# Inverse norms on VectorE by Newton steps instead of logarithms and exponentials on ScalarE, in a fused attention and feed-forward kernel

## The chip, the cores and the metric

The kernel runs on one core of a Trainium2 chip. The metric is the device time of one execution in microseconds (us). A core has five engines that run side by side and meet at semaphores: PE (TensorE, matrix products), DVE (VectorE), ACT (ScalarE, with activation tables that must be loaded), POOL (GpSimd) and SP (SyncE, which here only issues DMAs). Each engine works through its own list in order; an instruction that waits holds up all that stand behind it on its engine.

## The reference

The program is cosine attention followed by a feed-forward block with the gate h·cos(h):

```python
def _attn_ref(q, k, v, tau):                      # (8, 12, 448, 64) each
    q_n = q / (np.linalg.norm(q, axis=-1, keepdims=True) + 1e-06)
    k_n = k / (np.linalg.norm(k, axis=-1, keepdims=True) + 1e-06)
    scores = np.matmul(q_n, k_n.transpose(0, 1, 3, 2)) / tau
    scores = scores - np.max(scores, axis=-1, keepdims=True)
    attn = np.exp(scores)
    attn = attn / (np.sum(attn, axis=-1, keepdims=True) + 1e-09)
    return np.matmul(attn, v).astype(np.float32)

x = attn_out.transpose(0, 2, 1, 3).reshape(8 * 448, 768)
h = x @ w_in                                      # 768 x 2048
out = (h * np.cos(h)) @ w_out                     # 2048 x 768
```

The part of interest is the first two lines: each row of 64 numbers of q and k is divided by its norm plus 1e-6.

## The kernel before

**Quads.** The 96 heads are worked off as 24 quads of four heads (three quads make one of the eight batches). A quad holds 28 row norms per partition for q and k together: 14 for each, in the tile `n2` (sums of squares) and `rr` (inverse norms). Both tiles, and the scratch tile `nrm`, have two buffers, used by even and odd quads.

**Way of a quad through the engines.** SP loads `Qf` and `Kf` (L398). POOL squares them (`square`, L450), DVE sums the squares over 64 (L454, into `n2`). `inverse` (L461) makes `rr` from `n2`. POOL multiplies (`scale`, L501, into `Qn` and `Kn`), SP transposes both by DMA (`turn`, L544), and PE can then run the seven groups of scores of this quad (L560). ACT takes the exponential of each group into `E` (L567), PE multiplies `E` with V (L577), and DVE empties the one pair of PSUM banks used for that into `AVs` (L586) before the next quad may use it. Every second quad `sums` (L630) adds up the rows of `E` on PE, ACT inverts them by a logarithm and an exponential (L649, L651) and issues their store (L652), SP reads them back spread over the partitions (`R`, L658), and POOL (one quad: DVE) forms the normalised `xT` (L662).

**Inverse norm before the change.** All quads begin with ln and exp(0.5·) on ACT (L480, L483): that is the norm. Quads 1 to 7 (`FAST = 7`) then add 1e-6 by a reduction over pairs on DVE (L486) and take the reciprocal there (L489). Quad 0 and quads 8 to 23 stay on ACT: ln(norm + 1e-6) and exp(-·) (L491, L493). So ACT runs two instructions for each of quads 1 to 7 and four for each of quads 8 to 23.

**Stages.** The first three quads form a prologue whose order is written out by hand. From then on the program alternates, for each batch of 448 tokens, between a stage of the first product (`m1_part` and `m1`: PE L676, then per pair of 128 rows of h: ACT L689, DVE L691, ACT L693, DVE L695, which together compute h·cos(h) into `gT`), and a stage in which the second product (`m2`, L704, with its result copied out by DVE at L722) is mixed with the attention of the next quads: 5, 4, 3, 3, 3 and 3 of them, and none in the last two. PE pairs of L676 use four double PSUM banks in turn, so PE writes pair 4 only when DVE has finished L695 of pair 0; which pair frees which bank is given by `at_bank` (L921): for the first batch pairs 0, 2, 1 and 3 free the banks of pairs 4, 5, 6 and 7.

**Order of work.** PE's order is the order of the program text. The order on ACT, DVE, POOL and SP comes from a planner (class `Planner`) that goes through the operations with an assumed duration for each (the second argument of `op`), a latency after it (DVE 0.085) and a hop to the waiting engine (DVE 0.035), and at each point takes the operation that can start first; among those that can start together the one that is needed earliest goes first, and one needed over 1 us (`WORTH`) earlier is preferred. `lead` makes an operation count as needed so much earlier: 5 us for norms of quads 5 and on. An operation waits for an earlier one of its own engine by semaphore too, PE excepted.

**Where norms are asked for.** Quads 3 and 4 at L910 and L912, behind the last ACT instruction of the prologue (L609); that is at the start of the first m1 stage. Quad 5 at L981, in the first attention stage. Quads 6 to 23 by `begin` (L750), called at the first group of the quad two before, behind the exponential of the last group ahead of it.

Of the kernel before, what the change touches and what calls it, by code (L numbers as in the profile page):

```python
# [9 lines left out]
ALU = mybir.AluOpType  # L10
# [3 lines left out]
I32 = mybir.dt.int32  # L14
# [7 lines left out]
class Planner:  # L22
# [10 lines left out]
    FIRST, LAST = 1.2, 0.8  # L33
# [9 lines left out]
    def op(self, eng, dur, fn, r=(), w=(), after=(), dma=None, moves=0, mode="f", chain=None, keep=False, lead=0.0):  # L43
        o = Op()
        o.i, o.eng, o.dur, o.fn, o.dma, o.moves, o.mode, o.chain = (
            len(self.ops), eng, dur, fn, dma, moves, mode, chain)
        o.lat = self.FIRST + moves + self.LAST if dma else self.LAT[eng]
        o.behind, o.lead = None, lead
        if keep or self.strict and eng in ("act", "dve", "pool"):
            o.behind, self.tail[eng] = self.tail.get(eng), o  # L50
        o.reads, o.writes = tuple(r), tuple(w)
        deps = {a.i for a in after if a is not None}
        for x in o.reads:
            if x in self.last_write:
                deps.add(self.last_write[x].i)
        for x in o.writes:
            if x in self.last_write:
                deps.add(self.last_write[x].i)
            deps.update(p.i for p in self.readers.get(x, ()))
        deps.discard(o.i)  # L60
        o.deps = sorted(deps)
        for x in o.reads:
            self.readers.setdefault(x, []).append(o)
        for x in o.writes:
            self.last_write[x] = o
            self.readers[x] = []
        self.ops.append(o)
        return o
# [203 lines left out]
def bass_cosine_attention__then__act_gcu_kernel(  # L272
# [12 lines left out]
    NJ = S // D  # L285
# [6 lines left out]
    FIRST = 3  # L292
# [8 lines left out]
    def ring(name, n, shape, dt):  # L301
        return [sb("%s%d" % (name, i), shape, dt) for i in range(n)]
# [10 lines left out]
    n2 = ring("n2", 2, [128, 4 * NJ], F32)  # L313
    nrm = ring("nrm", 2, [128, 4 * NJ, 2], F32)
    rr = ring("rr", 2, [128, 4 * NJ], F32)
# [26 lines left out]
    op = P.op  # L342
# [24 lines left out]
    def table(m):  # L367
        if mode[0] == m:
            return
        mode[0] = m  # L370
        op("act", 1.3, lambda e: e.add_instruction(mybir.InstLoadActFuncSet(
            name=nc.get_next_instruction_name(), act_func_set_id={"exp": 6, "sin": 9}[m], engine=e.engine)),
           w=["table"])

    def act(m, dur, fn, r=(), w=(), **kw):
        table(m)
        return op("act", dur, fn, r=[*r, "table"], w=w, **kw)

    ALL = ((0, NJ),)
# [3 lines left out]
    def cut(kind, u, part):  # L383

        return [(kind, u, i) for i, (j0, j1) in enumerate(CELLS) if part[0] < j1 and j0 < part[1]]
# [39 lines left out]
        return pool_dma(0.79, lambda e: e.dma_start(W2.ap()[:, 8 * i:8 * i + 8, HW * hf:HW * hf + HW], src),  # L425
                 w=[("W2", i, hf)], dma=("W2", i, hf), moves=5.18)

    H, NLEAD, FAST = 2 * NJ, 5.0, 7
    SPARE = FIRST + 3

    def jr(t, w, part, off=0):
# [2 lines left out]
    def square(qd, w, eng, part=ALL[0], after=()):  # L434
# [23 lines left out]

        return add

    def inverse(qd, w0, w1, part=ALL[0], after=()):  # L461

        u = qd % 2
        ws = range(w0, w1)

        def cells(name):
            return [c for w in ws for c in cut("%s%d" % (name, w), u, part)]

        j0, j1 = part
        rows = [NJ, 2 * (w1 - w0)], [1, j1 - j0]
        if part == ALL[0]:
            rows = [[1, H * (w1 - w0)]]
        t, o = (bass.AP(x[u], w0 * H + j0, [[2 * H, 128], *rows]) for x in (n2, rr))
        wide = [[2 * a, b] for a, b in rows]
        z = bass.AP(nrm[u], 2 * (w0 * H + j0), [[4 * H, 128], *wide])
        both = bass.AP(nrm[u], 2 * (w0 * H + j0), [[4 * H, 128], *wide, [1, 2]])
        lead = NLEAD * (qd > FIRST + 1)
        act("exp", 0.12, lambda e: e.activation(z, t, ACT.Ln, bias=1e-30, scale=1.0), r=cells("n2"), w=cells("nrm"),  # L480
            after=after, lead=lead)
        yield
        act("exp", 0.12, lambda e: e.activation(z, z, ACT.Exp, bias=0.0, scale=0.5), r=cells("nrm"), w=cells("nrm"), lead=lead)  # L483
        yield
        if 0 < qd <= FAST:
            op("dve", 0.13, lambda e: e.tensor_reduce(out=o, in_=both, axis=AX.X, op=ALU.add), r=cells("nrm") + ["eps"],  # L486
               w=cells("rr"), lead=lead)
            yield
            op("dve", 0.27, lambda e: e.reciprocal(o, o), r=cells("rr"), w=cells("rr"), lead=lead)  # L489
            return  # L490
        act("exp", 0.12, lambda e: e.activation(z, z, ACT.Ln, bias=1e-6, scale=1.0), r=cells("nrm"), w=cells("nrm"), lead=lead)  # L491
        yield
        act("exp", 0.12, lambda e: e.activation(o, z, ACT.Exp, bias=0.0, scale=-1.0), r=cells("nrm"), w=cells("rr"), lead=lead)  # L493
# [15 lines left out]
    def norm_b(qd, eng="pool", after=()):  # L509
        for _ in inverse(qd, 0, 2, after=after):  # L510
            pass
        for w in range(2):
            last = scale(qd, w, eng)
        return last
# [278 lines left out]

    square(0, 1, "dve", KP[0])()
    key = inverse(0, 1, 2, KP[0])
    adds = []
    for part in QP:
# [10 lines left out]
    scale(0, 1, "dve", KP[0])  # L808
    adds[2]()
    query, key = inverse(0, 0, 1), inverse(0, 1, 2, KP[1])  # L810
    for x in (query, query, query, query, key, key, key, key):
        next(x, None)
# [213 lines left out]
```

## Time and profile before

| | |
|---|---|
| median of 3 runs | 441.71 us (440.83 to 442.9) |
| the profiled execution | 441.8 us, span 439.6 us, mean granted TensorE clock 0.992 |
| PE busy | 420.1 us (96%) |
| ACT busy | 315.3 us (72%), 434 instructions |
| DVE busy | 254.7 us (58%), 300 instructions |
| POOL busy | 211.2 us (48%), 145 instructions |
| ln and exp of the norms on 28 columns (L480, L483, L491, L493) | 23 + 23 + 16 + 16 instructions, 229, 228, 228 and 226 ns each |
| reduction and reciprocal on DVE (L486, L489) | 7 + 7 instructions, 200 and 326 ns each |
| exponentials of the scores (L567) | 168 instructions, 144.8 us in all |
| loads of activation tables (L371) | 16, 1283 ns each |

"Busy" counts the union of an engine's instructions; overlapping neighbours on DVE and ACT start about 0.1 us before the one ahead has ended. The time outside the span (2.2 us in the profiled execution) is start and end of the program. A line such as "PE PS L577 <- ACT E L567: 1.8, 7, 0.4" says that PE stood idle before L577 for 1.8 us in 7 places, the longest 0.4 us, and that ACT's L567 ended each of these waits.

### The profile page before, as it was taken

The page shows a single profiled execution, that of the slowest core. Times are in us where ns is not written, and L with a number is a line of the kernel's source. Part 1 is how long each engine was busy: PE and PEld are TensorE (multiplying, and loading weights), DVE is VectorE, ACT ScalarE, POOL GpSimd, SP SyncE. Part 2 cuts the span into 40 slices and gives each one's busy share as a digit, 9 for nine tenths or more (in the row PEclk, how much of TensorE's full clock was granted, in tenths as well). Part 3 has the DMA queues.
Part 4 walks back from the last instruction along what each step waited for, and adds up shares of the span by engine and source line. Part 5 has one row for each costly group of instructions (what it writes and reads, how often), then busy time and mean ns, then how long its engine had stood idle before and what let it go on. Part 6 is the DMA issues. An engine that isn't in the chain of part 4 may idle for free.

```text
span 439.6 us, 8369 instructions
## 1 busy us (share of the span) xinstructions
PE 420.1 (96%) x3544; PEld 204.6 (47%) x3544; DVE 254.7 (58%) x300; ACT 315.3 (72%) x434; POOL 211.2 (48%) x145
## 2 busy tenths in 40 slices
PE   5989999988999999999999999999999999999996
PEld 5444543324544345434554444434454445555553
DVE  4674995347863449823696419923585237825931
ACT  4798789896788877788688667888678666815700
POOL 3878727869167694376637682148633120030000
PEclk9699999999999999999999999999999999999999
DMA  7999996999919969188933994075912611051022
GB/s 253 233 251 227 261 196 92 233 223 208 146 41 240 240 172 213 37 206 123 265 89 80 241 210 141 1 171 150 259 35 48 154 43 30 0 159 36 1 71 73
DMA packets 70941, 64.34 MB, mean 146 GB/s; under 512 B 40100, under 2 KB 63224, under 8 KB 70904
## 3 DMA queue, kind: packets, MB, share of 16 engines
q1 hardware_dynamic: 57824, 51.30, 46.6%
q0 software_dynamic: 12288, 11.80, 18.2%
q10 hardware_dynamic: 792, 0.71, 0.5%
q8 instruction: 28, 0.46, 0.4%
q14 instruction: 9, 0.07, 0.1%
HBM read 55.25 MB, written 11.16 MB: 151 GB/s over the span
## 4 chain that ended last, share of the span: by engine, by line
PE 83%; ACT 9%; DVE 3%; issue 2%; POOL 2%; ACTq 1%; POOLq 0%
PE PS L676 33%; PE PS L704 31%; PE PS L560 7%; PE PS L577 6%; ACT E L567 6%; PE PS L642 4%; DVE n L454 1%; ACT Zs L651 1%; ACT Zs L649 1%; ACTq L652 1%; PE PS L599 1%; PE PS L623 1%; POOL xT L662 0%; DVE gT L695 0%; ACT ar L609 0%
## 5 line engine op out<-in xcount | busy, mean ns | idle before, releaser
L704 PE MATMUL PS<-W,gT 128*128 128x384 bf16 x896 | 163.4, 327 | 1.1 <-DVE osb L722 1.0
L567 ACT ACTIVATE E<-PS 128x896 bf16<-128x896 f32 x168 | 144.8, 916 | 27.0 <-PE PS L560 23.8
L676 PE MATMUL PS<-xT,W 128*128 128x448 bf16 x768 | 147.7, 353 | 1.2 <-POOL xT L662 1.2
L704 PEld LDWEIGHTS PS<-W,gT 128*128 128x128 bf16 x896 | 80.1, 98 | 80.7 <-issue 29.0
L676 PEld LDWEIGHTS PS<-xT,W 128*128 128x128 bf16 x768 | 74.3, 98 | 72.0 <-POOL xT L662 1.6
L689 ACT ACTIVATE ar<-PS 128x896 int32<-128x896 f32 x64 | 58.2, 910 | 45.1 <-PE PS L676 45.1
L691 DVE SCALAR_TENSOR_TENSOR ar<-ar,PS 128x896 f32<-128x896 int32 x64 | 69.2, 1083 | 29.0 <-ACT ar L689 29.0
L722 DVE COPY osb<-PS 128x384 f32<-128x384 f32 x54 | 29.2, 554 | 86.6 <-PE PS L704 86.5
L662 POOL TENSOR_TENSOR xT<-AVs,R 128x896 bf16<-128x896 f32 x20 | 41.4, 2088 | 67.5 <-DMA R<-rscr 67.4
L695 DVE TENSOR_TENSOR gT<-PS,ar 128x896 bf16<-128x896 f32 x64 | 69.6, 1088 | 1.5 <-ACT ar L693 1.0
L693 ACT ACTIVATE ar<-ar 128x896 f32<-128x896 f32 x64 | 60.6, 946 | 13.1 <-DVE ar L691 13.1
L560 PE MATMUL PS<-qT,kT 64*64 64x448 bf16 x672 | 62.1, 368 | 4.9 <-ACT E L567 4.0
L450 POOL TENSOR_TENSOR sqq<-Qf 128x896 bf16<-128x896 f32 x21 | 35.3, 1679 | 49.3 <-DVE n L454 40.9
L577 PE MATMUL PS<-E,Vb 64*64 64x448 bf16 x672 | 50.4, 353 | 2.1 <-ACT E L567 1.8
L501 POOL TENSOR_TENSOR Qn<-Qf,rr 128x896 bf16<-128x896 f32 x21 | 35.4, 1687 | 29.6 <-ACT rr L493 25.1
L450 POOL TENSOR_TENSOR sqk<-Kf 128x896 bf16<-128x896 f32 (+1 forms) x22 | 36.5, 1659 | 25.9 <-DVE n L454 17.9
L586 DVE COPY AVs<-PS 128x896 f32<-128x896 f32 x21 | 22.8, 1087 | 29.6 <-PE PS L577 29.6
L501 POOL TENSOR_TENSOR Kn<-Kf,rr 128x896 bf16<-128x896 f32 (+1 forms) x22 | 37.5, 1705 | 0.5 <-DVE Qn L501 0.5
L560 PEld LDWEIGHTS PS<-qT,kT 64*64 64x64 bf16 x672 | 18.6, 105 | 38.4 <-issue 15.6
L454 DVE TENSOR_REDUCE n<-sqq 128x14 f32<-128x896 bf16 (+2 forms) x24 | 24.9, 1037 | 5.8 <-POOL sqq L450 5.7
L454 DVE TENSOR_REDUCE n<-sqk 128x14 f32<-128x896 bf16 (+2 forms) x24 | 25.0, 1040 | 5.4 <-POOL sqk L450 5.4
L577 PEld LDWEIGHTS PS<-E,Vb 64*64 64x64 bf16 x672 | 19.3, 106 | 17.5 <-ACT E L567 10.6
(53 smaller groups left out, 175.9 us busy)
## 6 DMA issues: line engine op xcount, KB each, us to landing
Qf<-in_q_dram SPq DMA_DIRECT2D x24, 448.0 KB, 6.0
out_dram<-osb SPq DMA_DIRECT2D x54, 192.0 KB, 3.6
Kf<-in_k_dram SPq DMA_DIRECT2D x23, 448.0 KB, 7.2
R<-rscr SPq DMA_DIRECT2D x42, 224.0 KB, 4.2
Vb<-in_v_dram POOLq DMA_DIRECT2D x24, 224.0 KB, 6.7
W<-in_moe_w_in_dram POOLq DMA_DIRECT2D x4, 768.0 KB, 18.3
W<-in_moe_w_out_dram POOLq DMA_DIRECT2D x4, 768.0 KB, 31.9
Kf<-in_k_dram ACTq DMA_DIRECT2D x1, 320.0 KB, 6.2
```

Source lines behind the costliest of these rows:

```text
L450: op(eng, (1.68 if eng == "pool" else 1.05) * n, lambda e: e.tensor_tensor(dst, src, src, ALU.mult), r=cut(nm + "f", s, part), w=at, after ...
L454: return op("dve", 0.07 + 0.95 * n, lambda e: e.tensor_reduce(out=n2[u].ap()[:, H * w:H * w + H] if part == ALL[0] else jr(n2[u], w, part) ...
L501: lambda e: e.tensor_tensor(n[u].ap()[:, j0:j1].rearrange("p j r d -> p r j d"), f[s].ap()[:, :, j0:j1], rb, ALU.mult),
L560: ins = e.matmul(bank(bs + r, S, 64 * a, 64 * a + 64), kT[u].ap()[64 * r:64 * r + 64, j, a, :], qT[u].ap()[64 * r:64 * r + 64, :, a, :], s ...
L567: act("exp", 0.875, lambda e: e.activation(E[es].ap(), two(bs), ACT.Exp, bias=0.0, scale=INV_TAU), r=pair(bs), w=[("E", es)], chain="E")
L577: ins = e.matmul(bank((X, Y)[a], S, 64 * r, 64 * r + 64), Vb[vs].ap()[64 * a:64 * a + 64, r, j, :], E[es].ap()[64 * a:64 * a + 64, r, :], ...
L676: ins = e.matmul(bank(bk + i2), W1.ap()[:, i, 128 * nb:128 * nb + 128], xT[c % 2].ap()[:, i, :], start=(i == 0), stop=(i == NKC - 1))
L689: op("act", 0.815, lambda e: e.activation(ar[s].ap().bitcast(I32), two(bk), ACT.Identity, bias=0.25, scale=INV2PI), r=bs, w=[("ar", s)])
L691: op("dve", 1.005, lambda e: e.scalar_tensor_tensor(ar[s].ap(), ar[s].ap().bitcast(I32), -2.0 * math.pi, two(bk), ALU.mult, ALU.add), r=bs ...
L693: act("sin", 0.86, lambda e: e.activation(ar[s].ap(), ar[s].ap(), ACT.Sin, bias=GUARD * math.pi / 2.0, scale=GUARD), r=[("ar", s)], w=[("a ...
L695: op("dve", 1.01, lambda e: e.tensor_tensor(gT.ap()[:, 2 * pr:2 * pr + 2, col:col + S], two(bk), ar[s].ap(), ALU.mult), r=bs + [("ar", s)] ...
L704: ins = e.matmul(bank(bk, HW), gT.ap()[:, f, col:col + 128], W2.ap()[:, f, HW * h:HW * h + HW], start=(f == 0), stop=(f == NNB - 1))
```

## The change

Quads 3 to 23 get their inverse norms from a new function, `newton`, on DVE alone; quads 1 and 2 keep two ACT instructions and the reduction and reciprocal, and quad 0 its four on ACT. `newton` takes a first guess of 1/sqrt(a) from the bits of `n2` (one instruction on integers), improves it by three Newton steps of three instructions each, forms the norm as a·y, adds 1e-6 and takes the reciprocal: 13 instructions on 28 columns, each of which needs the one before. The scratch for all quads is `nrm[0]`, so that the chains of two quads don't overlap. The planner is told 0.03 us for each instruction and 0.2 us for the reciprocal. Place in the program, `after` and `lead` stay as they were.

```diff
-    H, NLEAD, FAST = 2 * NJ, 5.0, 7
+    H, NLEAD = 2 * NJ, 5.0
...
+    def newton(qd, lead, after):
+
+        u = qd % 2
+        a, y = n2[u].ap(), rr[u].ap()
+        s, t = (bass.AP(nrm[0], H * 2 * i, [[4 * H, 128], [1, 2 * H]]) for i in range(2))
...
+        def step(fn, r, w, dur=0.03, **kw):
+            op("dve", dur, fn, r=r, w=w, lead=lead, **kw)
+
+        step(lambda e: e.tensor_scalar(y.bitcast(I32), a.bitcast(I32), -0.5, float(0x5F3759DF), ALU.mult, ALU.add),
+             n2s, rrs, after=after)
+        yield
+        for _ in range(3):
+            step(lambda e: e.scalar_tensor_tensor(s, a, BIG, y, ALU.min, ALU.mult), n2s + rrs, ss)
+            step(lambda e: e.scalar_tensor_tensor(t, s, -0.5, y, ALU.mult, ALU.mult), ss + rrs, ts)
+            step(lambda e: e.scalar_tensor_tensor(y, t, 1.5, y, ALU.add, ALU.mult), ts + rrs, rrs)
+            yield
+        step(lambda e: e.scalar_tensor_tensor(s, a, BIG, y, ALU.min, ALU.mult), n2s + rrs, ss)
+        step(lambda e: e.tensor_scalar(t, s, 1e-6, None, ALU.add), ss, ts)
+        step(lambda e: e.reciprocal(y, t), ts, rrs, 0.2)
...
         lead = NLEAD * (qd > FIRST + 1)
+        if qd >= FIRST:
+            assert part == ALL[0] and (w0, w1) == (0, 2)
+            yield from newton(qd, lead, after)
+            return
...
-        if 0 < qd <= FAST:
+        if qd:
```

## The prediction

> **What bounds the kernel now.** I read the busy shares by engine first, then the busy time by stage, then PE's waits, then the groups of the norm instructions, last the timelines around the places where PE stands still. By stage (start:end, length, busy us and instruction count of each engine, granted clock, DMA share, GB/s):
>
> ```profile
> 38.70:57.00 18.30, 18.30 (x103) 9.50 (x101) 14.67 (x18) 14.70 (x20) 12.37 (x8) 1.00 1.24 245
> 57.00:100.30 43.30, 38.93 (x429) 15.36 (x427) 24.50 (x33) 37.94 (x57) 27.89 (x19) 1.00 0.98 184
> 177.10:208.00 30.90, 29.75 (x318) 13.07 (x316) 14.76 (x17) 26.20 (x40) 18.79 (x12) 1.00 0.60 125
> 208.00:226.60 18.60, 18.60 (x103) 9.43 (x101) 14.53 (x15) 13.02 (x16) 11.56 (x7) 1.00 0.90 218
> ```
>
> PE is the bound. It is busy without a gap in the m1 stages (18.30 of 18.30, 18.60 of 18.60), and loses 4.4 us in the first attention stage (57 to 100.3) and 1.15 in a later one. DVE is at 80% in the m1 stages, which one may take for room; ACT at 88% in the first attention stage. What ends PE's gaps over the whole run (us in total, times, longest):
>
> ```profile
> PE PS L560 <- ACT E L567: 4.0, 8, 0.8
> ...
> PE PS L577 <- ACT E L567: 1.8, 7, 0.4
> ...
> PE PS L676 <- POOL xT L662: 1.2, 1, 1.2
> PE PS L704 <- DVE osb L722: 1.0, 3, 0.3
> ...
> PE PS L577 <- DVE AVs L586: 0.2, 1, 0.2
> ```
>
> Of the 5.8 us for `E`, the same view cut at 57 us gives 4.8 behind the prologue, the only part the change can reach. With 1.2 for `xT` that makes 6.0 us: more than 1.4% can't be won, whatever ACT is spared.
>
> **What is removed from ACT.** Two instructions for each of quads 3 to 7 and four for each of 8 to 23: 10 + 64 = 74.
>
> ```profile
> L480 ACT ACTIVATE nrm<-n 128x28 f32<-128x28 f32 x23 | 5.2, 229 | 5.4 <-DVE n L454 5.2
> ...
> L489 DVE RECIPROCAL rr<-rr 128x28 f32<-128x28 f32 x7 | 2.3, 326 | 0.2
> ...
> L486 DVE TENSOR_REDUCE rr<-nrm 128x28 f32<-128x56 f32 x7 | 1.4, 200 | 6.8 <-ACT nrm L483 6.8
> ```
>
> At 0.228 us each that is 16.9 us of ACT time, but it counts only where PE waits for an `E` that stood behind a norm. I went through PE's waits one by one on the timelines of PE and ACT:
>
> ```profile
> 61.63 1.73 ACT L567 ACTIVATE E<-PS 128x896 bf16<-128x896 f32 x2 [0.29 <-PE PS L560]
> 64.13 0.23 ACT L480 ACTIVATE nrm<-n 128x28 f32<-128x28 f32 x1 [0.78 <-DVE n L454]
> 64.40 0.23 ACT L483 ACTIVATE nrm<-nrm 128x28 f32<-128x28 f32 x1
> 64.53 4.37 ACT L567 ACTIVATE E<-PS 128x896 bf16<-128x896 f32 x5
> ```
>
> Here ACT holds the third `E` for the norm of quad 5, which waits for DVE's sums; PE stands still 0.67 us at 65.48 and 0.23 at 66.29: 0.90, gone with the change. The norm of quad 8 (92.15 to 93.15) costs PE 0.32 + 0.23 at 94.01 and 94.81, but these 0.55 are hidden anyway: PE then stands 1.18 us at 100.28 for `xT`. The chain of waits enters that `xT` by this norm (POOL's Qn at 93.22 waits for L493, two squares follow, `xT` at 98.15 without a gap), yet a second branch ends at the same time: sums on PE at 84.7, their store issued at 87.4, the reload issued by SP from 93.28, 4.2 us to landing by the median. And the new chain would give `rr` no earlier: DVE's sums for quad 8 end at 90.0, plus 3.1 (below) is 93.1. The waits at 74.50 (0.42) and 88.99 (0.76) follow the inversion of the sums and its store, not a norm. In the stages from 177 and 278 us ACT mixes two of a norm's steps into the inversion of the sums; PE waits 0.6 + 0.2 for the `E` behind it. Most of that wait is the inversion and its DMA issue, so I take 0.3 of each: 0.6. The gain is 0.9 + 0.6 = 1.5 us; its bounds are 0 and 6.0.
>
> **What is added to DVE.** The trace has no `scalar_tensor_tensor` or `tensor_scalar` on 28 columns. The scale by `rr` on DVE (L501) takes 426 ns for 256 columns and 1092 for 896, so 1.04 ns a column and about 160 ns that don't depend on size; 28 columns are then 0.19 us. The lower bound is the shortest reduction of 56 columns, 0.15, the upper one the reciprocal, 0.33. Dependent instructions follow 0.04 us after the end of the one before (41.13 + 0.20, then 41.37). So I take 0.23 from step to step, nearest to the reduction with its gap: a chain is 12 x 0.23 + 0.33 = 3.1 us, where quads 3 to 7 had 0.53 on DVE and the later ones nothing. In all 21 x 3.1 - 5 x 0.5 = 62 us of DVE time, spread over 340 us in which DVE is half idle. The planner counts 0.03 + 0.085 + 0.035 = 0.15 a step, so each planned step makes DVE 0.08 us later than planned.
>
> [...]
>
> **Where it falls on the path, 1: the first m1 stage.** Quads 3 and 4 become ready together at 40.1 us.
>
> ```profile
> 41.13 0.20 DVE L486 TENSOR_REDUCE rr<-nrm 128x28 f32<-128x56 f32 x1
> 41.37 0.33 DVE L489 RECIPROCAL rr<-rr 128x28 f32<-128x28 f32 x1
> 41.61 0.15 DVE L486 TENSOR_REDUCE rr<-nrm 128x28 f32<-128x56 f32 x1
> 41.80 0.33 DVE L489 RECIPROCAL rr<-rr 128x28 f32<-128x28 f32 x1
> 43.59 2.08 DVE L691 SCALAR_TENSOR_TENSOR ar<-ar,PS 128x896 f32<-128x896 int32 x2 [1.46 <-ACT ar L689]
> ...
> 47.69 2.20 DVE L695 TENSOR_TENSOR gT<-PS,ar 128x896 bf16<-128x896 f32 x2
> ```
>
> The first chain runs from 41.13 to 41.13 + 3.1 = 44.2. The planner thinks it ends at 41.13 + 12 x 0.15 + 0.32 = 43.25 and puts two steps of the second chain ahead of the first L691: 44.2 + 0.46 = 44.7 in place of 43.59, 1.1 us late. PE starts pair 5 at 38.71 + 5 x 18.28 / 8 = 50.14 and needs the bank of pair 2, whose L695 ends at 49.89: 0.25 of slack, so PE stands still 0.85 us. (Pair 4 has 1.07 of slack, pair 6 more.) The second chain has 10 steps and the reciprocal left, 2.6 us, and DVE's gaps up to the end of this stage are 0.27 + 0.35 + 0.18 = 0.8. The other 1.8 push L691 and L695 of the last pairs, the copies of `qT` and `kT` (done at 61.11, PE's L560 at 61.19) and the table load behind the last L693; half of it, 0.9, I put on the path, since part lies ahead of instructions that still have slack. Together +1.75, between 0 (all of it in gaps) and 2.7.
>
> **2: AVs at the turn of a quad.** A chain starts when the last `E` of a quad is done, just as PE finishes with the banks that DVE must copy to `AVs`; queued behind the waiting step are that copy and the copies of L722. DVE's copy ended 0.27 us before PE wanted the banks at 135.80, 0.44 before 194.37, and 0.05 after at 79.24. Eight steps fit into the 1.2 us between the `E` that ended at 133.2 and the copy at 134.44; at 0.08 late each that is 0.64. Quad turns in mid-stage without sums on PE to cover them: quads 5, 7, 9, 11, 13, 17, 19. Seven at 0 to 0.64; I take 0.14, as the copies also lose L486 and L489 ahead of them: +1.0, between 0 and 4.5. Copies of L722 have some 4 us until their bank's turn and cost nothing until that is used up.
>
> **3: what only moves.** `rr` comes 2 to 3 us later after its sums, so do POOL's two scales (1.7 each), the reloads of `Qf` and `Kf` that wait for them, and SP's two transposes with the stores queued behind. In the stage from 123 us the scales of quad 10 end at 131.9, the transposes are issued by 134 and land 4.1 later, and PE comes to quad 10 after 14 groups at about 141. Cost nothing with 3 us of cover; without it up to 3 us, once. POOL also loses time beside a DVE instruction with two operands in SBUF (Kn took 2.53 at 100.19 in place of 1.69, beside DVE's 1.43): 10 such steps of 0.19 at 0.84 / 1.43 are at most 1.1 us of POOL a chain, with POOL 48% busy.
>
> **Sum.** -1.5 + 1.75 + 1.0 = +1.25 on the profiled run of 441.8, whose span is 439.6 and which lies at the median (441.71): 443.0.
>
> **Rivals.** *B, faster.* The planner hides the chains of quads 3 and 4 and the steps never meet a copy; then ACT has room: 0.9 as above, 0.42 at 74.50, 0.55 if POOL and the reload both bring `xT` sooner, and 1.3 of the 1.9 that PE waits for `E` from 100 us on: -3.2, so 438.5. For it: ACT at 88% in the first attention stage. Against: only 0.25 us of slack at pair 5. *C, slower.* The copies to `AVs` come behind Newton steps at each turn, from the point where DVE is more than 0.27 to 0.44 late: 7 x 0.5 = 3.5, with the first m1 stage at 2.7 and the gain at 1.5: +4.7, so 446.5. For it: 0.08 us lost a step, 13 steps in a row. Against: DVE waits 86.5 us for PE before L722, so lateness is caught up. *N, nothing.* The exponentials spared lie beside a busy PE, the steps in gaps of DVE, and the planner shuffles both: 441.7.
>
> **How the numbers follow.** Forecast 0.38 (own range 441.3 to 444.8), C 0.24, B 0.20, N 0.18. A measurement of this kernel tells 0.5% (2.2 us) from no change. Faster by more: B, 0.20. Slower by more (above 443.9): C and 0.16 of the forecast, 0.40. Same: the rest, 0.40. The range leaves out the outer thirds of B and C: 438.8 to 447.5.
>
> **What would show it.** DVE's first L691 near 44.7 and a PE gap before L676 for L695 in the first m1 stage; steps 0.23 apart; no PE gap at 65.5; PE's waits for `AVs` above 0.2 us in all. I am wrong if steps follow at 0.15 or less, if quad 4's chain is moved so that PE waits for its transposes, or if PE's waits for `E` fall by over 3 us.

## The result and the profile after

The changed kernel takes 480.0 us (474.0 to 480.7) against 442.3 before: 1.0835 times, interval 1.078 to 1.089. Its profiled execution took 479.6 us with a span of 477.6. The page's first part and two of the stages (start:end, length, busy us and count of PE, PEld, DVE, ACT and POOL, granted clock, DMA share, GB/s), the first m1 stage and the attention stage behind it:

```profile
PE 431.9 (90%) x3544; PEld 207.1 (43%) x3544; DVE 325.6 (68%) x563; ACT 303.2 (63%) x360; POOL 211.3 (44%) x145
```

```profile
39.50:60.00 20.50, 15.72 (x74) 7.43 (x73) 18.90 (x33) 11.39 (x14) 9.08 (x6) 0.92 1.28 223
60.00:117.60 57.60, 47.16 (x451) 18.55 (x449) 38.47 (x83) 39.41 (x47) 29.61 (x20) 0.91 0.58 134
```

The span grew by 38.0 us. PE's idle time grew from 19.5 to 45.7 us (26.2), and its busy time from 420.1 to 431.9 (11.8) for the same 3544 matmuls: the mean granted clock fell from 0.992 to 0.970, and (1 - 0.970) x 477.6 - (1 - 0.992) x 439.6 = 10.8 us. The clock fell behind PE's gaps, as 0.91 and 0.92 in these two stages show, where the kernel before had 1.00. What ended PE's gaps (us in total, times, longest):

```profile
PE PS L606 <- DVE AVs L615: 18.3, 7, 5.4
PE PS L705 <- DVE gT L724: 6.3, 4, 2.8
PE PS L733 <- DVE osb L751: 3.0, 3, 1.7
PE PS L589 <- ACT E L596: 2.9, 6, 0.8
...
PE PS L606 <- ACT E L596: 0.9, 4, 0.2
```

The line numbers are those of the changed file: L606, L589, L705, L733 are the L577, L560, L676, L704 of before. Waits for ACT fell from 5.8 to 3.8 us; waits for DVE behind the prologue rose from 1.2 to about 30. The groups of the chain's instructions (count | busy us, mean ns of one) say why:

```profile
L478 DVE SCALAR_TENSOR_TENSOR nrm<-n,rr 128x28 f32<-128x28 f32 x63 | 21.4, 340 | 1.8
L479 DVE SCALAR_TENSOR_TENSOR nrm<-nrm,rr 128x28 f32<-128x28 f32 x63 | 16.2, 258 | 1.9
L480 DVE SCALAR_TENSOR_TENSOR rr<-nrm,rr 128x28 f32<-128x28 f32 x63 | 15.9, 253 | 1.9
L474 DVE TENSOR_SCALAR rr<-n 128x28 int32<-128x28 int32 x21 | 11.7, 561 | 3.1 <-ACT E L596 2.5
...
L482 DVE SCALAR_TENSOR_TENSOR nrm<-n,rr 128x28 f32<-128x28 f32 x21 | 3.9, 187 | 0.7
L483 DVE TENSOR_SCALAR nrm<-nrm 128x28 f32<-128x28 f32 x21 | 3.8, 180 | 0.7
```

L478 and L482 are the same instruction on the same tiles, 340 and 187 ns. An instruction of fixed size whose mean differs so much has a few long ones in it. DVE's timeline in the first m1 stage (start, us), and POOL's at the same time:

```profile
44.59 0.19 DVE L478 SCALAR_TENSOR_TENSOR nrm<-n,rr 128x28 f32<-128x28 f32 x1
44.81 1.56 DVE L479 SCALAR_TENSOR_TENSOR nrm<-nrm,rr 128x28 f32<-128x28 f32 x1
46.41 1.62 DVE L480 SCALAR_TENSOR_TENSOR rr<-nrm,rr 128x28 f32<-128x28 f32 x1
47.95 2.07 DVE L720 SCALAR_TENSOR_TENSOR ar<-ar,PS 128x896 f32<-128x896 int32 x2
```

```profile
44.65 1.68 POOL L530 TENSOR_TENSOR Qn<-Qf,rr 128x896 bf16<-128x896 f32 x1 [2.29 <-DVE rr L484]
46.30 1.68 POOL L530 TENSOR_TENSOR Kn<-Kf,rr 128x896 bf16<-128x896 f32 x1
```

A step of 28 columns lasts 1.6 us while POOL multiplies, and ends 0.04 and 0.05 us after POOL's instruction (46.33 and 47.98). POOL was set off by the first chain's own `rr`. In the whole run 20 steps are over 0.37 us; each ends 0.03 to 0.06 us behind the end of a POOL instruction. Over the 0.19 (0.18 for L474) that an undisturbed step takes, the four groups hold 63 x (0.15 + 0.07 + 0.07) + 21 x 0.38 = 26 us. A turn of a quad shows what follows from it. DVE, then PE:

```profile
90.90 0.19 DVE L479 SCALAR_TENSOR_TENSOR nrm<-nrm,rr 128x28 f32<-128x28 f32 x1
91.12 2.71 DVE L480 SCALAR_TENSOR_TENSOR rr<-nrm,rr 128x28 f32<-128x28 f32 x1
93.86 0.19 DVE L478 SCALAR_TENSOR_TENSOR nrm<-n,rr 128x28 f32<-128x28 f32 x1
93.97 1.08 DVE L615 COPY AVs<-PS 128x896 f32<-128x896 f32 x1
```

```profile
91.51 0.38 PE L589 MATMUL PS<-qT,kT 64*64 64x448 bf16 x4
95.10 0.96 PE L606 MATMUL PS<-E,Vb 64*64 64x448 bf16 x8 [3.21 <-DVE AVs L615]
96.37 1.14 PE L733 MATMUL PS<-W,gT 128*128 128x384 bf16 x3
```

POOL's product for `xT` runs from 91.69 to 93.77. The step waits for it, the copy of `AVs` stands behind the step, PE waits 3.21 us for the copy, and then works at half clock (granted 0.50 from 93.76 to 100.59): three L733 take 1.14 us, where three took 0.65 at 87.83.

### The profile page after: what moved, and what is told of

Same layout as the page of the kernel before. It is cut to its first block, busy times and chain, and to the rows that moved or that the text cites. A ratio compares the mean times of both kernels' runs of the same rounds, so it can differ in the third digit from the quotient of the medians.

```text
span 477.6 us, 8554 instructions
## 1 busy us (share of the span) xinstructions
PE 431.9 (90%) x3544; PEld 207.1 (43%) x3544; DVE 325.6 (68%) x563; ACT 303.2 (63%) x360; POOL 211.3 (44%) x145
## 4 chain that ended last, share of the span: by engine, by line
PE 51%; DVE 28%; POOL 8%; ACT 6%; issue 4%; DMA 2%; ACTq 0%; SPq 0%; POOLq 0%; DVEq 0%
PE PS L705 22%; PE PS L733 18%; DVE n L454 4%; DVE gT L724 4%; PE PS L589 4%; DVE nrm L478 3%; PE PS L606 3%; DVE ar L720 3%; ACT E L596 3%; DVE nrm L479 3%; DVE rr L480 2%; DVE rr L474 2%; DVE AVs L615 2%; POOL Qn L530 2%; POOL Kn L530 2%
## 5 line engine op out<-in xcount | busy, mean ns | idle before, releaser
L733 PE MATMUL PS<-W,gT 128*128 128x384 bf16 x896 | 167.3, 332 | 3.0 <-DVE osb L751 3.0
L705 PE MATMUL PS<-xT,W 128*128 128x448 bf16 x768 | 150.5, 355 | 9.3 <-DVE gT L724 6.3
L733 PEld LDWEIGHTS PS<-W,gT 128*128 128x128 bf16 x896 | 80.8, 99 | 85.9 <-issue 32.9
L705 PEld LDWEIGHTS PS<-xT,W 128*128 128x128 bf16 x768 | 74.3, 98 | 82.8 <-DVE gT L724 8.5
L720 DVE SCALAR_TENSOR_TENSOR ar<-ar,PS 128x896 f32<-128x896 int32 x64 | 69.0, 1081 | 21.2 <-ACT ar L718 21.2
L722 ACT ACTIVATE ar<-ar 128x896 f32<-128x896 f32 x64 | 60.6, 947 | 23.4 <-DVE ar L720 23.2
L606 PE MATMUL PS<-E,Vb 64*64 64x448 bf16 x672 | 52.0, 366 | 19.3 <-DVE AVs L615 18.3
L589 PE MATMUL PS<-qT,kT 64*64 64x448 bf16 x672 | 64.4, 379 | 4.5 <-ACT E L596 2.9
L691 POOL TENSOR_TENSOR xT<-AVs,R 128x896 bf16<-128x896 f32 x20 | 41.4, 2083 | 57.2 <-DMA R<-rscr 57.2
L589 PEld LDWEIGHTS PS<-qT,kT 64*64 64x64 bf16 x672 | 19.2, 108 | 41.0 <-ACT E L596 16.9
L454 DVE TENSOR_REDUCE n<-sqq 128x14 f32<-128x896 bf16 (+2 forms) x24 | 25.0, 1041 | 15.8 <-POOL sqq L450 15.6
L606 PEld LDWEIGHTS PS<-E,Vb 64*64 64x64 bf16 x672 | 19.1, 108 | 34.8 <-DVE AVs L615 20.4
L454 DVE TENSOR_REDUCE n<-sqk 128x14 f32<-128x896 bf16 (+2 forms) x24 | 24.9, 1040 | 2.5 <-POOL sqk L450 2.5
## 6 DMA issues: line engine op xcount, KB each, us to landing
Qf<-in_q_dram SPq DMA_DIRECT2D x24, 448.0 KB, 4.8
Kf<-in_k_dram SPq DMA_DIRECT2D x23, 448.0 KB, 5.6
```

The costliest lines, as they stand in the source:

```text
L454: return op("dve", 0.07 + 0.95 * n, lambda e: e.tensor_reduce(out=n2[u].ap()[:, H * w:H * w + H] if part == ALL[0] else jr(n2[u], w, part) ...
L589: ins = e.matmul(bank(bs + r, S, 64 * a, 64 * a + 64), kT[u].ap()[64 * r:64 * r + 64, j, a, :], qT[u].ap()[64 * r:64 * r + 64, :, a, :], s ...
L606: ins = e.matmul(bank((X, Y)[a], S, 64 * r, 64 * r + 64), Vb[vs].ap()[64 * a:64 * a + 64, r, j, :], E[es].ap()[64 * a:64 * a + 64, r, :], ...
L705: ins = e.matmul(bank(bk + i2), W1.ap()[:, i, 128 * nb:128 * nb + 128], xT[c % 2].ap()[:, i, :], start=(i == 0), stop=(i == NKC - 1))
L720: op("dve", 1.005, lambda e: e.scalar_tensor_tensor(ar[s].ap(), ar[s].ap().bitcast(I32), -2.0 * math.pi, two(bk), ALU.mult, ALU.add), r=bs ...
L722: act("sin", 0.86, lambda e: e.activation(ar[s].ap(), ar[s].ap(), ACT.Sin, bias=GUARD * math.pi / 2.0, scale=GUARD), r=[("ar", s)], w=[("a ...
```

## The experiments

Theory: DVE's steps with two operands in SBUF, and the integer step, wait for a running POOL instruction. Rival: 13 dependent steps are too long and planned too short, with or without POOL. The runs below bear the theory out: none of 252 reductions with one operand was held (one_input, 181 ns each), of 21 steps with two operands exactly the six were that began while POOL multiplied (one_pair, up to 1.94 us in place of 0.19), and of 21 integer steps nine were (integer_only, 550 ns on average over the 21 in place of 180). What makes a step wait no run shows.

The changed kernel has a control of its own. L720 is a `scalar_tensor_tensor` like the Newton steps, with one operand in SBUF and one in PSUM (ns min/median/max):

```profile
L720 DVE SCALAR_TENSOR_TENSOR ar<-ar,PS x64: 1028/1080/1089, 48.0 to 454.0; 128x896 f32<-128x896 int32 x64
```

14 of the 64 begin while POOL multiplies, and none is held. So the operation as such isn't what is held.

Times of before beside the runs were 441.7 to 442.6.

**one_input.** All twelve steps ahead of the reciprocal as reductions with one operand. The order on every engine is that of the changed kernel.

```diff
-        step(lambda e: e.tensor_scalar(y.bitcast(I32), a.bitcast(I32), ...), n2s, rrs, after=after)
+        step(one(y, ca), n2s, rrs, after=after)       # one: tensor_reduce over an axis of one element
...
-            step(lambda e: e.scalar_tensor_tensor(s, a, BIG, y, ALU.min, ALU.mult), n2s + rrs, ss)
+            step(one(s, ca), n2s + rrs, ss)
```

> Every chain of the changed kernel keeps its 13 instructions, their dependencies and their place in every engine's order, but the twelve ahead of the reciprocal become reductions over one element, with one operand in SBUF (the Newton steps are left out, the norms are not formed). Theory (a DVE instruction with two SBUF operands, or the integer one that starts a chain, is held until a running POOL instruction ends; this costs 26 us of DVE and with it PE's gaps): no step longer than 0.35 us, PE's waits for AVs below 4 us in all, time 440 to 448. Rival (the chain of 13 is simply too long, and planned too short, so that copies queue behind it): time 465 to 482, PE's waits for AVs above 12 us.

Measured: 449.2 us, 1.0165 (1.0129 to 1.0201). The groups of the steps, and PE's waits for DVE:

```profile
L475 DVE TENSOR_REDUCE nrm<-nrm 128x28 f32<-128x28 f32 x84 | 15.2, 181 | 2.7
L475 DVE TENSOR_REDUCE nrm<-n 128x28 f32<-128x28 f32 x84 | 15.2, 181 | 2.5
```

```profile
PE PS L610 <- DVE AVs L619: 5.9, 5, 2.8
...
PE PS L737 <- DVE osb L755: 1.6, 3, 0.6
...
PE PS L709 <- DVE gT L728: 0.7, 1, 0.7
```

Same number, same order, same spacing (0.22 us from step to step), and none is held, though 87 of the 252 reductions begin while POOL multiplies: 30.8 of the 37.7 us are gone. The time and the wait for `AVs` (5.9) are a little above the theory's bounds, so the rival has a part, some 7 us.

**planned_long.** The changed kernel with `dur=0.1` for `dur=0.03` in `step`.

> The changed kernel, with the planner told 0.10 us for each step in place of 0.03, so that a planned step takes 0.22 us as measured. Theory (held by POOL): held steps remain, some 15 to 25 of them with 20 to 30 us in all, and the time stays at 465 to 490. Rival (planned too short): time falls to 446 or less, PE's waits for AVs below 4 us.

467.3 us, 1.0565 (1.0529 to 1.0600). 22 steps are held for 29 us together; PE's waits for `AVs` fell to 10.8. A truer plan saves 13 us, but the holds stay. As the theory had it; the rival's 446 is far off.

**one_input_long** and **one_input_long_2.** Both edits together, in two runs of the same kernel; the profile is that of the second.

> As one_input (reductions with one operand in SBUF in place of the Newton steps, the norms are not formed), but planned with 0.10 us a step. Theory (the 7.3 us that one_input still lost are the planner's 0.07 us too few per step, which make copies to AVs late, and the half clock behind the gaps): 441 to 445, PE's waits for AVs below 1.5 us. Rival (the chain of 3 us is too long for the turn of a quad in any order): 447 to 450 as one_input.

> one_input_long once more (reductions in place of the Newton steps, 0.10 us a step in the plan; the norms are not formed), for a profile at full clock. 444 to 447; PE's waits for AVs below 2.5 us; what is left over before lies in PE gaps that follow chains, and in half clock behind them.

446.6 and 446.5 us, 1.0093 (1.0048 to 1.0138) and 1.0097 (1.0060 to 1.0134). PE's waits in the second:

```profile
PE PS L610 <- DVE AVs L619: 2.1, 2, 1.2
PE PS L593 <- DMA kT<-Kn: 1.6, 1, 1.6
PE PS L737 <- DVE osb L755: 1.6, 3, 0.6
PE PS L593 <- DVE kT L567: 1.5, 2, 1.3
```

With the plan put right, some 3 of the 7 us go, about 4.5 stay. So the expectation of the first (441 to 445) was too low: the chain's mere length costs something in any order tried, at turns (`AVs`) and now also because `kT` comes later. Half clock is no part of it here: the granted clock from 40 to 440 us is 1.00.

**quads_3_4** and **from_quad_5.** `if qd >= FIRST` narrowed to quads 3 and 4, and to `qd > FIRST + 1`, with `FAST` as before for the others. (In the first, the shared scratch overwrites the 1e-6 that quad 6 adds.)

> Newton chains for quads 3 and 4 alone, the others as before the change. In the changed kernel four held steps lie in the first m1 stage (1.56, 1.62, 1.48 and 0.42 us) and PE loses 4.8 us there. Theory: plus 4 to 9 us over before (446 to 451), with a stretch of half clock behind the PE gap. Rival (chain length as in the blind working, no hold): plus 0 to 2.7 us.

> Newton chains for quads 5 to 23, quads 3 and 4 as before the change. Theory: the rest of the loss, plus 25 to 33 us (467 to 475), PE's waits for AVs 12 to 20 us. If the two parts don't add up to the whole 38 us within 5 us, the parts interact (through the order of the plan or the clock). Rival (only the first m1 stage matters and shifts all that follows): below 446.

448.0 us, 1.0125 (1.0085 to 1.0164), and 467.5, 1.0563 (1.0519 to 1.0607): plus 6.1 and plus 25.6, both in the theory's ranges. Together 31.7 against 37.7 for both, 6 us short, so the parts interact somewhat; which of clock and plan does it wasn't taken apart. In quads_3_4 three steps are held for 4.2 us and PE waits 4.9 us for `gT` in the first m1 stage.

**integer_only.** one_input with the integer step put back.

> As one_input, in its order, but the first instruction of each chain is again the integer tensor_scalar of the change, SBUF to SBUF; the other eleven are reductions with one operand (the norms are not formed). In the changed kernel seven of these 21 were long, 7.9 us over their 0.18. [...] Rival (they were long in the changed kernel only because steps with two operands ran ahead of them): none above 0.35 us, time as one_input, 448 to 451.

456.4 us, 1.0338 (1.0307 to 1.0368), where I had expected 451 to 460 with 5 to 10 long steps. The group, one held step, and POOL at that time:

```profile
L479 DVE TENSOR_SCALAR rr<-n 128x28 int32<-128x28 int32 x21 | 11.5, 550 | 3.2 <-ACT E L601 2.6
```

```profile
157.46 1.31 DVE L479 TENSOR_SCALAR rr<-n 128x28 int32<-128x28 int32 x1
```

```profile
157.03 1.69 POOL L450 TENSOR_TENSOR sqq<-Qf 128x896 bf16<-128x896 f32 x1
```

Nine of 21 are long, 21 x (550 - 180) = 7.8 us in all. Eight end 0.04 to 0.05 us behind a POOL product (here 158.77 and 158.72), one with the issue of a DMA by POOL. One operand, but held: this form is an exception. Whether that is due to `tensor_scalar` from SBUF to SBUF or to the integers stays open, since the `tensor_scalar` on floats (L483) never began beside a POOL product in any run. The step stands at the head of a chain and costs 7 us over one_input, so the rival falls.

**one_pair.** one_input with the eleventh step of each chain a `scalar_tensor_tensor` on two SBUF operands.

```diff
-        step(one(s, ca), n2s + rrs, ss)
+        step(lambda e: e.scalar_tensor_tensor(s, a, 1.0, a, ALU.mult, ALU.max), n2s + rrs, ss)
```

> As one_input, in its order, but one of the twelve, the tenth-but-one, is a scalar_tensor_tensor with both operands in SBUF; all others are reductions (the norms are not formed). Theory: of 21 such steps those that begin while POOL multiplies are held, 4 to 12 of them, 3 to 10 us in all, time 450 to 458; all other steps stay at 0.18. Rival (a hold needs a train of such steps, or two different tiles): none above 0.35, time 448 to 451.

448.9 us, 1.0172 (1.0134 to 1.0210). The step by its tile (ns min/median/max), then the longest, and POOL:

```profile
L486 DVE SCALAR_TENSOR_TENSOR nrm<-n x21: 176/188/1942, 41.7 to 344.0; 128x28 f32<-128x28 f32 x21
```

```profile
302.59 1.94 DVE L486 SCALAR_TENSOR_TENSOR nrm<-n 128x28 f32<-128x28 f32 x1
```

```profile
300.36 4.12 POOL L695 TENSOR_TENSOR xT<-AVs,R 128x896 bf16<-128x896 f32 x2 [3.27 <-DMA R<-rscr]
```

Six of 21 began while POOL multiplied, and these six are the long ones, 3.4 us in all; the other 15 take 0.18 to 0.19. One step alone, on one tile twice, is enough for a hold. The time is that of one_input, so these 3.4 us cost PE nothing that can be told; whether because they are few or because they come near the end of a chain wasn't taken apart. The forecast of the holds was met, that of the time was not.

**pool_halves.** The changed kernel in its order, with each of POOL's products issued as two halves.

```diff
+    def halves(e, eng, part, o, x, y, cut_):
...
+        for i in range(2):
+            ins = e.tensor_tensor(cut_(o, i), cut_(x, i), cut_(y, i), ALU.mult)
+        return ins
```

> The changed kernel, whole and in the same order on every engine, but each of POOL's squares, scales and products for xT is issued as two instructions of half the size (before: 1.68 and 2.08 us each; by the prologue's 1.25 us for 640 columns a half takes about 0.93). Theory (a step waits for the end of the POOL instruction that runs): a hold begun in one half lasts at most about 1.05 us unless the next half gets in first; the total over the steps' own time falls from 26 to 10 to 18 us and the time to 455 to 470. Rival (a step waits until POOL has nothing to do, or POOL's work as such slows DVE): holds stay at 24 to 30 us in all, time 475 to 485.

475.0 us, 1.0733 (1.0685 to 1.0781).

```profile
L486 DVE SCALAR_TENSOR_TENSOR nrm<-nrm,rr 128x28 f32<-128x28 f32 x63 | 19.2, 305 | 1.9
L485 DVE SCALAR_TENSOR_TENSOR nrm<-n,rr 128x28 f32<-128x28 f32 x63 | 18.6, 296 | 1.8
```

Most holds are now 0.8 to 1.1 us, one half, and back to back: at 284.70 and 285.80 two steps are held 1.06 each, where one of 2.0 stood before. But there are 26 over 0.37 us in place of 20, and the total is 22 us: above what I expected, below the rival. The time missed my range too and lies at the lower end of the rival's. The rival's mechanism isn't borne out all the same: 22 of the 26 end with the half beside which they began, though often the next half follows at once. A step gets in between two POOL instructions and the next step is held by the next one. In the other four (1.3, 1.4, 1.6 and 2.9 us) POOL's next instruction came in first. So a hold is mostly the rest of one instruction, as the theory has it; the number of holds grew with the number of POOL's instructions (26 against 20), which I had left out.

**no_norms.** The kernel before without inverse norms from quad 3 on.

```diff
+        if qd >= FIRST:
+            return
         act("exp", 0.12, lambda e: e.activation(z, t, ACT.Ln, bias=1e-30, scale=1.0), ...
```

> The kernel before without any inverse norm from quad 3 on: neither ACT nor DVE works on them, POOL scales by values left from quads 1 and 2. It is the most that sparing ACT can bring. By the blind sum (1.5 us of PE's waits stand behind a norm) 440.0; by the faster rival 438.5; by the bound of all waits for E and xT 436. If it is above 441, ACT's norms cost nothing and the change had nothing to win.

442.05 us, 1.0021 (0.9985 to 1.0058). PE's waits behind the prologue, from 38 us on:

```profile
PE PS L562 <- ACT E L569: 1.9, 3, 0.8
PE PS L579 <- ACT E L569: 1.4, 5, 0.4
PE PS L706 <- DVE osb L724: 1.0, 3, 0.3
PE PS L678 <- DVE xT L664: 0.9, 1, 0.9
PE PS L678 <- POOL xT L664: 0.7, 1, 0.7
```

Over the whole run PE's waits for `E` fall from 5.8 to 3.8 us, just as in the changed kernel. Behind the prologue they fall from 4.7 to 3.3, and those for `xT` grow from 1.2 to 1.6 (the plan's order differs too). The time stays: by the interval, 0.7 us at most could be won, less than half of the 1.5 predicted.

**two_on_act.** `FAST = 23` in the kernel before.

> The kernel before with its mixed way (two instructions on ACT, then a reduction and a reciprocal on DVE, one SBUF operand each) for all quads from 1 on, in place of quads 1 to 7: ACT is spared 32 instructions, 7.3 us, and DVE gets 16 x 0.53 = 8.5 us. Theory (no_norms at 442.05 shows that sparing ACT brings nothing, and one-operand instructions aren't held): 441 to 443.5, the same as before. Rival (ACT's last two instructions do cost, and only the Newton chain hid it): 438.5 to 440.

442.7 us, 1.0004 (0.9986 to 1.0021): the same. The reduction and the reciprocal have one SBUF operand each. It spares ACT 32 instructions and neither wins nor loses. No version tried is faster than the kernel before.

## Why the prediction was wrong

*PE is the bound, little can be won.* Right, and too generous: of the 1.5 us of gain, no_norms leaves 0.7 at most.

*What a step costs.* 0.23 us from step to step was predicted, 0.22 measured, 0.187 of it the step, when POOL is quiet. The planner's 0.15 was the right suspicion.

*The first m1 stage.* L691 was to start at 44.7 us and PE to lose 0.85 us. Without holds (one_input) it starts at 44.95 and PE loses 0.66. With them it starts at 47.95, and PE loses 2.84 and 1.95.

*AVs at the turn of a quad.* The place was right, the term mis-sized even without holds: 1.0 us was put on it, 4.5 at most; one_input lost 5.9 - 0.2 = 5.7 there. I had taken at most eight steps of 0.08 as the delay, while the copy can stand behind a whole chain: in one_input it waits for 13 instructions from 71.62 to 74.55, behind two sums of 2.19 us, and PE stands still 2.85 us for it. With holds the waits are 18.3.

*The step that failed* is in part 3: "POOL also loses time beside a DVE instruction with two operands in SBUF", at most 1.1 us a chain and of no account. The price was put on POOL, while DVE's steps were bounded by 0.33 us each. Measured, POOL lost nothing (211.2 us busy before, 211.3 after) and DVE's steps were held for 26 us, 20 of them 0.4 to 2.7 us long. None of the three signs of being wrong came (steps 0.22 apart, no wait of PE for a transpose, waits for `E` down by 2.0 us), so the prediction had no sign for this. I had the row that tells it all and read it one way. These are the lines of the kernel before, DVE's and POOL's:

```profile
99.75 1.43 DVE L662 TENSOR_TENSOR xT<-AVs,R 128x896 bf16<-128x896 f32 x1
```

```profile
98.15 2.08 POOL L662 TENSOR_TENSOR xT<-AVs,R 128x896 bf16<-128x896 f32 x1
100.19 2.53 POOL L501 TENSOR_TENSOR Kn<-Kf,rr 128x896 bf16<-128x896 f32 x1
```

DVE's product takes 1.43 in place of 1.09 because it starts while POOL's runs until 100.23; POOL's next takes 2.53 in place of 1.69 because DVE's runs until 101.18. I made a rate of it, 0.84 us lost per 1.43 us of overlap, and shrank it to 28 columns. It is a wait: here, as in the 20 long steps, the one that came second waited for the rest of the other's instruction, whatever its own size (28 or 896 columns). (The changed kernel has the pair again: DVE's product for `xT` starts at 117.33, and POOL's square at 117.56 takes 2.53.) For a step of 0.19 us against POOL's 1.68 and 2.08 the price is up to ten times the step, on DVE and not on POOL. POOL is busy 48% of the time; one hold in each chain's reach, priced at half a POOL instruction, would have put an estimate of 21 x 0.85 = 18 us of DVE time in the sum. Apart from that one product, what the kernel before does on DVE in its stages keeps clear of this: L691, L695, L722, L586, the reductions and the reciprocals have one operand in SBUF or read PSUM. Of the 64 L691 before, 19 begin while POOL multiplies, and the longest of all takes 1.09 us; of the 64 L695 it is 13 and 1.09, of the 54 L722 31 and 0.56, of the 21 L586 10 and 1.09, of the 50 sums L454 21 and 1.09, of the 7 reductions L486 3 and 0.21, of the 7 reciprocals one and 0.33.

*The rivals.* C, copies behind Newton steps, was the right place and sign; its price (446.5) was bounded by the same 0.08 us a step, and so the range was. B and N fell.

Where the 37.7 us went: holds 30.8 (480.0 against 449.2 in the same order, the half clock behind them included), the planner's short steps about 3 (449.2 against 446.5), the chain's length in a better plan about 4.5 (446.5 against 442). The first two depend on the order in which they are taken: with the plan put right first, that saves 13 us (480.0 to 467.3) and the holds cost 21 (467.3 against 446.5), so about 10 us come from holds and a short plan together. The split between PE's waits and clock, 26.2 and 11.8, cuts across these.

## What to carry to other kernels

Before an instruction is moved to DVE, count its operands in SBUF and look what POOL does at that time: here a small instruction with two operands in SBUF cost the rest of a POOL instruction (0.4 to 2.7 us in place of 0.19), and what stood behind it in DVE's queue paid. One operand wasn't always safe: the integer step was held as well (nine of 21 in integer_only). Where two engines lengthen each other in a trace, check first whether one ends just after the other (here 0.03 to 0.06 us); then it is a wait, to be priced by the other's length and not by overlap. And measure the prize first: leaving the work out altogether (no_norms) would have shown that there was 0.7 us at most.

## What the runs showed that was not expected

A step was held beside a DMA issue of POOL too: in integer_only the step at 41.71 took 0.41 us and ended with the issue of a load of V (41.38 to 42.14). The step held longest in the changed kernel (2.71 us at 91.12) began during such an issue (90.95 to 91.67), and POOL's product came in ahead of it. And the clock made PE's gaps dearer by almost half: 26.2 us of waits brought 11.8 us of slower matmuls with them, while quads_3_4, with one pair of gaps in the first m1 stage, shows 423.0 us of PE time against 420.1. The trace of the changed kernel shows the clock halved: behind the prologue the granted clock is 0.50 in five stretches, 20.5 us in all, with PE busy for 18.7 of them, which makes about 9 of the 11.8 us. Two of them (the form is that of the stages above):

```profile
56.22:59.63 3.41, 3.41 (x11) 1.40 (x10) 3.38 (x7) 1.90 (x2) 0.60 (x1) 0.50 1.28 207
...
93.76:100.59 6.83, 5.49 (x36) 1.79 (x36) 2.79 (x9) 2.75 (x3) 4.36 (x4) 0.50 0.69 190
```

Each begins in a PE gap of 1.95 to 5.44 us or within 0.8 us of its end. None begins in the gap of 2.84 us at 48.35 or in the 5 us behind it, so the length of a gap alone doesn't tell here whether one follows.
